# Order and queues of the opening loads, and a weight fold turned into 64-row passes, in a fused attention and feed-forward block

## The chip, the cores and the metric

The program runs on one core of one Trainium2 chip. The metric is the device time of one execution in microseconds (us). A profiled execution gives the trace; its span is the stretch that the trace covers. Engines are written PE (TensorE, matmul), PEld (TensorE weight load, which overlaps PE), ACT (ScalarE), DVE (VectorE), POOL (GpSimd) and SP (SyncE). Of these, SP and ACT issue DMAs here, each into a queue of its own; SPq and ACTq in the trace are those issues.

## The reference

x is 2048 tokens by 448. A layer norm of x feeds two branches, and the result is x plus both:

```
x = A_x;  xn = layernorm(x)
return x + A(xn, A_wqkv, A_w_phi, A_wo) + B(xn, B_w1, B_w2)

def A(x, wqkv, w_phi, wo):            # H = 16 heads of Dh = 28
    q, k, v = split(x @ wqkv)
    pq = einsum("bhsd,hdf->bhsf", q, w_phi);  pk = the same of k
    phi_q = concat(softmax(pq), softmax(-pq));  phi_k = the same of pk
    kv = einsum("bhsf,bhsd->bhfd", phi_k, v);  z = sum over s of phi_k
    num = einsum("bhqf,bhfd->bhqd", phi_q, kv);  den = einsum("bhqf,bhf->bhq", phi_q, z) + 1e-6
    return merge_heads(num / den) @ wo
def B(x, w1, w2): return silu(x @ w1) @ w2        # 448 -> 1792 -> 448
```

The head map w_phi (16 matrices of 28x28) acts on q and k only through the product wqkv times w_phi, so the kernel forms that product once, which is called the fold, and multiplies tokens by the folded weight.

## The kernel before, in words

Tokens are cut into 16 tiles of 128. The kernel does not run its loops on the engines directly: it records operations (`P.op`, `P.dma`), tracks what each reads and writes, and a list scheduler (L218) with a cost for every operation sets the order on each engine. That order is then emitted with semaphore waits. PE's order is fixed by hand: a head that is written out word by word in a `chain`, and after it the string `PLAN` (L334). In PLAN, `aF3@4` and `bF3` are the two halves of feed-forward block 3 into PSUM banks 4 and 5, `av2`, `ak2`, `aq2` the same for v, k and q of tiles 2 and 3, `f2@24` a part of the fold, `K0-2` the kv product, `M` its masking, `Y` and `F` with a small number the second feed-forward matmul of a tile, `U` the product of phi_q with kv, and `W`, `R`, `E` the output projection and store. Work of 64 rows is done as pairs, two matmuls in the two halves of the array into two banks.

**Opening loads (L505 to L555).** SP's queue issues x of tile 0, of tile 1, of tiles 2 and 3, then w1 columns 0 to 511 (two loads, called w1_0 and w1_0r here), the last rows of w1 columns 512 to 1023, x of tiles 4 to 7, the rest of w1, wv, x of tiles 8 to 11, and x of 12 to 15. ACT's queue issues the head map (Wp, 56 bytes a row) and then the main part of w1 columns 512 to 1023 (w1_512). The order on SP behind x of tiles 8 to 11 is written out in a chain (L931): three of the eight transposing loads of wqkv (wT_dma0 to 2, L580), x of 12 to 15, the transposes of normalised tiles 4 to 7 (xnT_dma5 and 7), the other five of wqkv, the transposes of tiles 8 to 15, w2 and wo.

**Head.** DVE normalises tiles 0 to 3 in the order of a chain (L893): statistics of tiles 0 and 1 come before the scale of tile 0. PE transposes them, ACT or DVE moves them back to SBUF, and PE starts feed-forward blocks 0, 1 and 2 tile by tile (L905 to L919). Tile 4 and later tiles are transposed by DMA. Blocks 5 and 6 of the next 512 tokens (F12, F13) are the first to read them.

**Fold (L568 to L597).** POOL spreads the head map into block-diagonal form, 112 rows by 4 times 112 (BDphi). For each of four row blocks of wqkv (kt), eight matmuls of 112 rows by 112 columns multiply transposed wqkv with it. `f2@24` does row blocks 2 and 3, `f0@24` row blocks 0 and 1, 16 matmuls each. For each kt, ACT copies the last column of each head (last27), and one DVE subtraction of 864 elements a partition writes Wqk without that column; the kernel uses that a softmax does not change under a common shift. The transposed wqkv lies in the space of Y_sb, which is written much later.

Of the kernel before, what the change touches and what calls it, by code (L numbers as in the profile page):

```python
# [140 lines left out]
class _Prog:  # L141
# [76 lines left out]
    def schedule(self):  # L218
# [55 lines left out]
        while done < n:  # L274
# [58 lines left out]
          ("pool", "pe"): 100.0}  # L333
PLAN = """aF3@4 bF3 aF6@0 aF4@2 bF4 bF6 av2@4 aF5@6 bv2 bF5 av0@2 aF12@0 aF13@4 bv0 bF12 bF13 aF11@6 bF11 f2@24 aF8@0 aF10@6 bF8  # L334
bF10 f0@24 aF9@0 aF7@6 bF9 bF7 ak2@4 bk2 av12@6 ak14@2 bv12 av10@0 bk14 bv10 ak4@4 av14@6 bk4 ak0@2 bv14 ak8@0 bk0 bk8
av6@6 Y2@5:1 Y2:9 Y2:4 ak6@2 av8@0 bv6 bv8 bk6 av4@6 ak10@4 bv4 bk10 ak12@2 aq4@0 bk12 K0-2 bq4 aq6@4 K2-4 bq6 aq8@2
K4-6 bq8 aq0@0 aF17@4 s4 K6-10 bq0 aF14@2 bF17 bF14 aF19@0 K10-12 bF19 aF16@4 K12-16 aF23@2 bF16 bF23 aF27@0 aF24@4 bF27
bF24 M aF20@2 aF25@0 bF20 aF15@4 bF25 aF26@2 aF22@6 bF26 aF18@0 s6 s8 bF22 bF15 bF18 aq2@6 aF21@2 aq10@4 bF21 bq2 aq12@0
bq10 bq12 F7@3:8 Y0@6:7 U9 Y1@5:6 F6@4:14 Y1:3 s0 F9@2:11 U6@1 Y1:5 U5 U7@0 Y0:7 F9:3 s2 Y3@1:10 Y3:4 W9 s10 s12 U10
U3@5 W6 F7:6 aq14@0 R9,6 bq14 U8 W7 F5@4:8 s14 F10@5:7 U0 F10:7 U11@6 U12@1 F5:6 U4@2 F4@0:10 W5 F8@7:12 W10 F4:4 F8:2  # L340
U2@1 W4 W0@6 W3@2 W8 R4,3 R8 R0,7,10,5 F13@1:14 F11@2:3 F12@6:4 F14@5:7 W2@3 U1@4 U13 F14:7 F11:2 F11:3 F12:1 F11:4 U14
F11:1 F11:1 W11 W1@4 F12:9 W12 U15 W13 W14 R14,12 R13,11 R1,2 F15@07:5 F15:5 F15:4 E15"""


def bass_parallel_sum__linear_kernel_hedgehog__dense_activation_silu__prompt_kernel(
# [12 lines left out]
    KP = 112  # L358
# [17 lines left out]
    with es:  # L376
        def sb(name, shape, dt):
            return es.enter_context(nc.sbuf_tensor(name, shape, dt))
# [12 lines left out]
        DQ = H * DF  # L391
        Wqk = sb("Wqk", [128, 2, 4, DQ], BF16)
        last27 = sb("last27", [128, 4, 2, H], F32)
        Wp = sb("Wp", [KP, G, DH], BF16)
        BDphi = sb("BDphi", [KP, G, KP], BF16)

# [23 lines left out]
        ones_bf = sb("ones_bf", [128, 128], BF16)  # L420
        ones4 = sb("ones4", [KP, 4], F32)
        mtmp = sb("mtmp", [KP, 4], F32)
        maskh = sb("maskh", [KP, 4], F32)
        mask2 = sb("mask2", [KP, 2], F32)
# [37 lines left out]
        def d_pool(n, per=1.0):  # L462
            return n * per + 120.0
# [35 lines left out]
        def load(dst, src, name, eng="sp", lat=1700.0):  # L499
            n = 2  # L500
            for _, cnt in list(dst.ap):
                n *= cnt
            P.dma(lambda e: e.dma_start(out=dst, in_=src), n / 280.0, writes=[dst], name=name, eng=eng, lat=lat)  # L503

        load(Wp[:], A_w_phi.rearrange("(g hl) d f -> (hl d) g f", g=G), "wphi", eng="act", lat=2500.0)  # L505
        memset(ones_bf[:], 1.0, 128, "ones")
# [5 lines left out]
        memset(ones4[:], 1.0, 4, "ones4")  # L512
        act(warm_act[:], ones_bf[:, 0:4], ACTF.Sqrt, 1750, "warm_act", table="sqrt")

        def block_mask(dst, w, n):
            tmp = mtmp[:, 0:n]
            P.op("pool", d_pool(4), lambda e: e.affine_select(tmp, ones4[:, 0:n], [[-w, n]], ALU.is_ge, 0.0,
                                                               base=0, channel_multiplier=1),
                 reads=[ones4[:]], writes=[tmp], name="mask1")
            P.op("pool", d_pool(4), lambda e: e.affine_select(dst, tmp, [[w, n]], ALU.is_ge, 0.0,  # L520
                                                               base=w - 1, channel_multiplier=-1),
                 reads=[tmp], writes=[dst], name="mask2")

        block_mask(maskh[:], DH, 4)

# [6 lines left out]

        def load_x(t0, t1):
            load(x_sb[:, t0:t1, :], xt[:, t0:t1, :], f"x{t0}", lat=1400.0)

# [4 lines left out]
        def load_w1(c0, c1, eng="sp"):  # L540
            load_rows4(w1_sb[:, :, c0:c1], B_w1, c0, c1, f"w1_{c0}", eng)

        load_x(0, 1)
        load_x(1, 2)
        load_x(2, 4)
        load(w1_sb[:, 0:2, 0:512], B_w1[0:256, 0:512].rearrange("(k p) f -> p k f", p=128), "w1_0")
        load(w1_sb[:, 2:4, 0:512], bass.AP(B_w1.tensor, B_w1.offset + 256 * FF, [[FF, 128], [64 * FF, 2], [1, 512]]), "w1_0r")
        load_w1(512, 1024, "act")
        load_x(4, 8)
        load_w1(1024, FF)  # L550
        load_rows4(wv_sb, A_wqkv, 2 * D, 3 * D, "wv")
        load_x(8, 12)
        load_x(12, 16)
        load(w2_sb[:], B_w2.rearrange("(f p) d -> p f d", p=128), "w2")
        for i in range(2):  # L555
# [9 lines left out]

        bd4 = BDphi[:].rearrange("p g (h f) -> p g h f", h=4)

        def fold():  # L568
            P.op("pool", d_pool(448, 2.0), lambda e: e.tensor_tensor(
                bd4, Wp[:, :, None, :].broadcast_to([KP, G, 4, DH]),  # L570
                maskh[:, None, :, None].broadcast_to([KP, G, 4, DH]), ALU.mult),
                reads=[Wp[:], maskh[:]], writes=[BDphi[:]], name="bdphi")

        def fold_loads():
            for a in range(8):
                dma_t(wT_sb[:, a, :], A_wqkv[:, a * KP:a * KP + 128], 600.0, f"wT_dma{a}", 1800.0 if a == 2 else 1310.0, sbuf=False)

        def fold_mms(k0, slots):
            mms = []
            for kt, fb in zip((k0, k0 + 1), slots):  # L580
                for qk in range(2):
                    wps = banks[fb + qk][:, 0:G * KP].rearrange("p (g c) -> p g c", g=G)
                    mms += [(wps[:, g, :], wT_sb[0:KP, qk * 4 + g, KS[kt]:KS[kt] + 128], BDphi[:, g, :], True, True) for g in range(G)]
            P.cur_slack = 400.0
            pe_mms(mms, "fold", dur=50.0 * len(mms))
            P.cur_slack = 0.0
            for kt, fb in zip((k0, k0 + 1), slots):
                src = psum[:, fb * 512:(fb + 2) * 512].rearrange("p (b c) -> p b c", b=2)[:, :, 0:D].rearrange("p b (h f) -> p b h f", f=DH)
                ref = last27[:, kt, :, :]
                act(ref, src[:, :, :, DF], ACTF.Identity, 32, "fold_ref")  # L590
                dst = Wqk[:, :, kt, :].rearrange("p b (h f) -> p b h f", f=DF)
                fold_sub(dst, src[:, :, :, 0:DF], ref)

        def fold_sub(dst, src, ref):
            P.op("dve", d_dve(2 * DQ), lambda e: e.tensor_tensor(dst, src, ref[:, :, :, None].broadcast_to([128, 2, H, DF]), ALU.subtract),
                 reads=[src, ref], writes=[dst], name="fold_sub")
# [119 lines left out]
        def proj_block(t, b0, is_k):  # L716
            fns = pair_block(b0, DQ, lambda i, kt, r: xnT[r, t + i, kt, :],
                             lambda i, kt, r: Wqk[r, int(is_k), kt, :], "k" if is_k else "q")

            def evac():  # L720
                E2 = ek(t, 2)[:, :, 0:2 * D] if is_k else eq(t, 2)
                src = psum[:, b0 * 512:(b0 + 2) * 512].rearrange("p (i c) -> p i c", i=2)[:, :, 0:DQ].rearrange("p i (h f) -> p i h f", f=DF)
                dst = E2.rearrange("p i (h s f) -> p i h s f", s=2, f=DH)
                for sg in range(2):
                    act(dst[:, :, :, sg, 0:DF], src, ACTF.Exp, 2 * DQ, "exp", scale=(1.0 if sg == 0 else -1.0), table="exp", okeys_w=["acttab"])
                E4 = E2.rearrange("p i (h f) -> p i h f", f=DH)
                R2 = Rec[:, int(is_k), t:t + 2, :]
                step = 2 if is_k else 1
                for i in range(0, 2, step):
                    sums(E4[:, i:i + step], R2[:, i:i + step, :], step)  # L730
                if is_k:
                    scale_rows(t, is_k)

            return *fns, evac
# [158 lines left out]
        chain("bnst0 bnag0 bnst1 bnag1 rstd0 xn0a xn0 rstd1 xn1 bnst2 bnag2 bnst3 bnag3 rstd2 xn2 rstd3 xn3 ev3".split())  # L893
        chain("wphi warm_act w1_512 ve0 ve1 ev0a ev0 ev1 ve2 ve3 ev2 silu_table".split())
        fold_loads()
# [24 lines left out]
        chain("ev3 bnst4".split())  # L920
        block_mask(mask2[:], 2 * DH, 2)
        memset(vaug[:, :, :, DH], 1.0, 2150, "vaug1")
# [6 lines left out]
        for t in range(8, NT):  # L929
            ln_tile(t)  # L930
        chain("x8 wT_dma0 wT_dma1 wT_dma2 x12 xnT_dma5 xnT_dma7 wT_dma3 wT_dma4 wT_dma5 wT_dma6 wT_dma7 xnT_dma9 xnT_dma11 xnT_dma13 xnT_dma15 w2 "  # L931
              "wo0 wor0 wo1 wor1".split())
# [18 lines left out]
        for word in PLAN.split():  # L951
# [10 lines left out]
            elif kind == "f":  # L962
                k0, slots = arg.split("@")
                fold_mms(int(k0), tuple(map(int, slots)))
            elif kind == "K":
# [141 lines left out]
```

The softmax here doesn't subtract the row's maximum and nothing guards it: scores larger than these inputs give would overflow.

## Time and profile before

| what | value |
|---|---|
| time before, median of 4 runs | 149.99 us |
| lowest and highest run | 149.33 and 151.0 us |
| the profiled execution's own time | 151.0 us |
| its span in the trace | 149.7 us |
| granted TensorE clock | 1.0 |
| HBM read, written | 6.56 MB, 1.84 MB |

The table's own-time row is one of the four runs, so 1.3 us of it lie outside the span and it is 1.0 us above the median. DVE is busy for 60% of the span, ACT for 47%, POOL for 48%. The busy time of POOL is concentrated in the middle, where it scales phi_k and phi_q. Lines of the page and the views give a start, a duration, the engine, the source line, the tiles written and read, and in brackets the idle time just before with what ended it. Times in the views count from the start of the span.

### The profile page before, as it was taken

How to read it: one execution, taken by the hardware profiler on the slowest of the kernel's cores; microseconds unless marked ns; L12 is line 12 of the kernel's file. 1: busy time of each engine (PE TensorE's matmuls, PEld its weight loads, DVE VectorE, ACT ScalarE, POOL GpSimd, SP SyncE). 2: the span in 40 equal slices, each digit the busy share in tenths (PEclk: the TensorE clock that was granted, in tenths of full speed). 3: DMA queues.
4: the chain of work that ended last, by engine and by line, in shares of the span. 5: the costliest groups of instructions: out<-in, count | busy, mean ns of one | idle time of the engine just before them, and what ended most of it. 6: DMA issues, size and time to landing. Idle time of an engine off the chain costs nothing.

```text
span 149.7 us, 3656 instructions
## 1 busy us (share of the span) xinstructions
PE 145.6 (97%) x1540; PEld 80.8 (54%) x1540; DVE 90.4 (60%) x189; ACT 70.8 (47%) x88; POOL 71.4 (48%) x82
## 2 busy tenths in 40 slices
PE   7899999999999999999999999999999999999994
PEld 7686444454554456566444444555545655455563
DVE  1839899344199949702997002999377902825284
ACT  3436775655999399969755769600003000000000
POOL 7105467701049999999699900599000800000000
PEclk9999999999999999999999999999999999999999
DMA  4999984899900000000078860038889348532325
GB/s 101 353 375 206 190 179 77 165 165 343 276 6 4 0 0 7 0 4 0 4 139 122 163 125 15 4 72 172 154 105 194 72 73 169 138 120 43 66 65 185
DMA packets 44352, 17.42 MB, mean 116 GB/s; under 512 B 36912, under 2 KB 43952, under 8 KB 44336
## 3 DMA queue, kind: packets, MB, share of 16 engines
q1 hardware_dynamic: 41168, 14.99, 48.4%
q10 hardware_dynamic: 3168, 2.20, 4.7%
q8 instruction: 12, 0.20, 0.6%
q14 instruction: 4, 0.03, 0.1%
HBM read 6.56 MB, written 1.84 MB: 56 GB/s over the span
## 4 chain that ended last, share of the span: by engine, by line
PE 92%; DMA 4%; SPq 1%; DVE 1%; issue 0%
PE psum L469 92%; DMA phT<-in_B_w_dram 4%; SPq L503 1%; DVE x_sb L855 1%; PE psum L484 0%
## 5 line engine op out<-in xcount | busy, mean ns | idle before, releaser
L469 PE MATMUL psum<-xnT,phT 64*128 64x512 bf16 (+1 forms) x428 | 46.9, 355 | 0.4
L469 PE MATMUL psum<-w_sb,hT 128*128 128x448 bf16 (+1 forms) x238 | 45.2, 342 | 0.0
L737 DVE TENSOR_REDUCE Rec<-Ek_sb 128x32 f32<-128x896 bf16 (+1 forms) x20 | 24.3, 1247 | 26.8 <-ACT Ek_sb L489 19.2
L773 POOL TENSOR_TENSOR RA<-Ek_sb,Rec 128x896 bf16<-128x896 bf16 x16 | 27.0, 1724 | 21.1 <-DVE Rec L738 19.7
L489 ACT ACTIVATE hT<-psum 128x1024 bf16<-128x1024 f32 x28 | 27.3, 1023 | 13.2 <-PE psum L469 13.2
L469 PEld LDWEIGHTS psum<-xnT,phT 64*128 64x128 bf16 (+1 forms) x428 | 21.8, 97 | 21.5 <-PE psum L469 1.7
L469 PEld LDWEIGHTS psum<-w_sb,hT 128*128 128x128 bf16 x238 | 22.3, 98 | 18.7 <-issue 1.5
L489 ACT ACTIVATE Ek_sb<-psum 128x864 bf16<-128x864 f32 x24 | 20.2, 932 | 17.4 <-DVE x_sb L855 16.1
L469 PE MATMUL psum<-Wqk,xnT 64*128 64x432 bf16 x224 | 23.7, 343 | 0.1
L747 POOL TENSOR_TENSOR Ek_sb<-Ek_sb,Rec 128x896 bf16<-128x896 bf16 x8 | 13.4, 1703 | 9.1 <-ACT phT L489 9.1
L469 PEld LDWEIGHTS psum<-Wqk,xnT 64*128 64x128 bf16 x224 | 10.4, 95 | 10.1 <-PE psum L469 0.8
L747 POOL TENSOR_TENSOR phT<-phT,Rec 128x896 bf16<-128x896 bf16 x8 | 13.4, 1706 | 0.0
L469 PE MATMUL psum<-wv,xnT 64*128 64x448 bf16 x112 | 12.7, 349 | 0.0
L602 DVE BATCH_NORM_STATS2 st<-x_sb 128x6 f32<-128x448 bf16 x16 | 9.7, 605 | 3.5 <-DMA x_sb<-in_A_x_dram 3.5
L469 PE MATMUL psum<-wo_sb,vaug 128*128 128x448 bf16 (+1 forms) x51 | 11.0, 341 | 0.0
L833 DVE TENSOR_SCALAR den<-psum 128x16 f32<-128x16 f32 x16 | 2.4, 157 | 13.4 <-PE psum L469 13.4
L840 DVE TENSOR_TENSOR vaug<-psum,rden 128x448 bf16<-128x448 f32 x16 | 9.8, 623 | 0.4
L489 ACT ACTIVATE vaug<-psum 128x896 bf16<-128x896 f32 x8 | 7.4, 934 | 5.1 <-PE psum L469 5.0
L617 DVE TENSOR_SCALAR RA<-x_sb,mv,rstd 128x384 bf16<-128x384 bf16 (+4 forms) x29 | 8.9, 344 | 1.4 <-POOL rstd L613 1.2
L855 DVE TENSOR_TENSOR x_sb<-psum,x_sb 128x448 bf16<-128x448 f32 (+1 forms) x13 | 7.1, 582 | 2.9 <-PE psum L469 2.9
L738 DVE RECIPROCAL Rec<-Rec 128x32 f32<-128x32 f32 (+1 forms) x24 | 8.6, 391 | 0.1
L469 PEld LDWEIGHTS psum<-wv,xnT 64*128 64x128 bf16 x112 | 5.5, 94 | 5.2
(51 smaller groups left out, 107.6 us busy)
## 6 DMA issues: line engine op xcount, KB each, us to landing
out_dram<-x_sb ACTq DMA_DIRECT2D x15, 112.0 KB, 1.8
w_sb<-in_B_w_dram SPq DMA_DIRECT2D x1, 1568.0 KB, 7.5
x_sb<-in_A_x_dram SPq DMA_DIRECT2D x3, 448.0 KB, 6.9
wo_sb<-in_A_wo_dram SPq DMA_DIRECT2D x2, 336.0 KB, 8.4
phT<-in_B_w_dram SPq DMA_DIRECT2D x1, 576.0 KB, 8.0
phT<-in_B_w_dram SPq DMA_DIRECT2D x2, 256.0 KB, 5.6
phT<-in_B_w_dram ACTq DMA_DIRECT2D x1, 384.0 KB, 4.6
wv<-in_A_wqkv_dram SPq DMA_DIRECT2D x1, 336.0 KB, 8.4
```

The lines of the kernel that those rows point to most:

```text
L469: r = e.matmul(dst, lhsT, rhs, start=st, stop=sp, skip_group_check=True)
L489: P.op("act", d_act(n), lambda e: e.activation(dst, src, func, scale=scale), reads=[src], writes=[dst], table=table, name=name, **keys)
L503: P.dma(lambda e: e.dma_start(out=dst, in_=src), n / 280.0, writes=[dst], name=name, eng=eng, lat=lat)
L602: P.op("dve", 590, lambda e: e.bn_stats(st6[:, t, :], xs), reads=[xs], writes=[st6[:, t, :]], name=f"bnst{t}", okeys_w=["ln"])
L617: P.op("dve", dur, lambda e: e.tensor_scalar(dst, x_sb[:, t, c0:c1], mv[:, t, 0:1], rstd[:, t:t + 1], ALU.subtract, ALU.mult), reads=[xs, ...
L737: P.op("dve", 50 + 967 * n, lambda e: e.tensor_reduce(R2, E4, AXL.X, ALU.add), reads=[E4], writes=[R2], name="Ssum")
L738: P.op("dve", 135 + 210 * n, lambda e: e.reciprocal(R2, R2), reads=[R2], writes=[R2], name="Rrec")
L747: P.op("pool", 1700, lambda e: e.tensor_tensor(E3, E3, Rk[:, :, None].broadcast_to([128, 32, DH]), ALU.mult), reads=[E3, Rk], writes=[E3], ...
L773: P.op("pool", 1700, lambda e: e.tensor_tensor(dst, Eq, Rq.rearrange("p (c j) -> p c j", c=CC)[:, :, :, None].broadcast_to([128, CC, 4, DH ...
L833: P.op("dve", 190, lambda e: e.tensor_scalar(den[:, uq, :], U3[:, :, DH], EPS_DEN, None, ALU.add), reads=[U3[:, :, DH]], writes=[den[:, uq ...
L840: P.op("dve", 620, lambda e: e.tensor_tensor(o3, U3[:, :, 0:DH], rden[:, uq, :, None].broadcast_to([128, H, DH]), ALU.mult), reads=[U3[:, ...
L855: P.op("dve", d_dve(cs.stop - cs.start), lambda e: e.tensor_tensor(res[:, cs], ob, addend[:, cs], ALU.add), reads=[ob, addend[:, cs]], wri ...
```

## The change

It does four things.

1. Tile 1 of x goes out on ACT's queue, as its first DMA; SP's queue starts with tile 0 and goes on to tiles 2 and 3. The main part of w1 columns 512 to 1023 moves from ACT's queue to SP's, behind w1_0 and w1_0r.
2. The head map is no longer loaded first on ACT's queue, but by four DMAs in SP's queue (one of 112 partitions with three pieces of 56 bytes each, three of 56 partitions with one piece), behind x of tiles 12 to 15 and ahead of xnT_dma5.
3. The fold is done in passes of 64 rows and 56 columns (two heads). wqkv is transposed by nine DMAs (NW = 9) whose columns overlap so that each half of a tile holds two whole heads. Each kt then takes nine matmuls in the low half of the array and seven in the high half, into two banks. Four words `f0`, `f3`, `f2`, `f1` of PLAN do one kt each. PW is 56. Every kt has two ACT copies and three DVE subtractions (54, 432 and 378 elements). POOL makes two smaller block-diagonal tiles and two more masks.
4. PLAN is new. The first fold word comes after six more pairs of feed-forward matmuls than before, and the order of Y, F, U, W and R words in the last third differs; the amount of that work does not.

```diff
-        load(Wp[:], A_w_phi.rearrange("(g hl) d f -> (hl d) g f", g=G), "wphi", eng="act", lat=2500.0)
...
         load_x(0, 1)
-        load_x(1, 2)
+        load_x(1, 2, "act")
         load_x(2, 4)
...
-        load_w1(512, 1024, "act")
+        load_w1(512, 1024)
...
         load_x(12, 16)
+        phi = A_w_phi.rearrange("h d f -> (h d) f")
+        P2 = 2 * DH
+        load(Wp[8:8 + KP, 0:3, :], phi[P2:P2 + 3 * KP, :].rearrange("(g p) f -> p g f", g=3), "wphi")
+        load(Wp[8:64, 3, :], phi[D - P2:D, :], "wphi1")
+        load(Wp[64:64 + P2, 3, :], phi[0:P2, :], "wphi2")
+        load(Wp0[0:P2, :], phi[0:P2, :], "wphi3")
...
         def fold_loads():
-            for a in range(8):
-                dma_t(wT_sb[:, a, :], A_wqkv[:, a * KP:a * KP + 128], 600.0, f"wT_dma{a}", 1800.0 if a == 2 else 1310.0, sbuf=False)
+            for i in range(NW):
+                c = max(0, KP * i - 64)
+                dma_t(wT(i), A_wqkv[:, c:c + 128], 600.0, f"wT_dma{i}", 1800.0 if i == 2 else 1310.0, sbuf=False)
...
-                    mms += [(wps[:, g, :], wT_sb[0:KP, qk * 4 + g, KS[kt]:KS[kt] + 128], BDphi[:, g, :], True, True) for g in range(G)]
+                mms.append((banks[b][:, PW * i:PW * i + PW], w[lo], BD[lo, (i - 1) % G, :] if i else BD0[:], i == 0, i == NW - 1))
+                if 0 < i < NW - 1:
+                    mms.append((banks[b + 1][:, PW * (i - 1):PW * i], w[hi], BD[hi, (i - 1) % G, :], i == 1, i == NW - 2))
...
-        chain("wphi warm_act w1_512 ve0 ve1 ev0a ev0 ev1 ve2 ve3 ev2 silu_table".split())
+        chain("x1 warm_act ve0 ve1 ev0a ev0 ev1 ve2 ve3 ev2 silu_table".split())
...
-        chain("x8 wT_dma0 wT_dma1 wT_dma2 x12 xnT_dma5 xnT_dma7 wT_dma3 wT_dma4 wT_dma5 wT_dma6 wT_dma7 xnT_dma9 xnT_dma11 xnT_dma13 xnT_dma15 w2 "
+        chain("x8 wT_dma0 wT_dma1 wT_dma2 x12 wphi wphi1 wphi2 wphi3 xnT_dma5 xnT_dma7 wT_dma3 wT_dma4 wT_dma5 wT_dma6 wT_dma7 wT_dma8 xnT_dma9 xnT_dma11 xnT_dma13 xnT_dma15 w2 "
```

The two PLAN strings up to the first k block, the old one first:

```
aF3@4 bF3 aF6@0 aF4@2 bF4 bF6 av2@4 aF5@6 bv2 bF5 av0@2 aF12@0 aF13@4 bv0 bF12 bF13 aF11@6 bF11 f2@24 aF8@0 aF10@6 bF8 bF10 f0@24 aF9@0 aF7@6 bF9 bF7 ak2@4
aF3@4 bF3 aF4@0 aF6@2 av2@6 bF4 bF6 aF5@4 av0@0 bv0 bF5 aF12@2 bv2 aF11@0 aF13@4 bF12 bF11 bF13 aF10@6 aF8@0 f0@2 f3@4 bF8 bF10 f2@2 aF9@0 f1@4 aF7@6 bF9 bF7 ak2@4
```

## The prediction

> **What bounds the kernel now.** I read the page's busy times and slices first, then the chain of work in order of time, then the timeline of the opening, and last the timelines of PE and of SP's queue where the change touches them.
>
> ```profile
> PE 145.6 (97%) x1540; PEld 80.8 (54%) x1540; DVE 90.4 (60%) x189; ACT 70.8 (47%) x88; POOL 71.4 (48%) x82
> ...
> PE   7899999999999999999999999999999999999994
> ```
>
> PE is busy in every slice but the first two and the last, so the only time to be won is PE work itself, the opening, and the end. The chain says where PE waited:
>
> ```profile
> 2.67 6.42 DMA phT<-in_B_w_dram
> 9.09 0.05 issue
> 9.14 0.98 PE psum L469 x8
> ...
> 26.91 9.64 PE psum L469 x102
> 36.55 0.04 issue
> 36.60 110.69 PE psum L469 x1184
> ```
>
> Columns are start, length and what. The last wait of PE on anything but itself ends at 9.14 us, with the load w1_0r (issued at 2.67). From there to 147.3 us PE has no gap worth a tenth: whatever a new order adds as a wait is paid in full, and whatever PE work goes is gained in full. The opening:
>
> ```profile
> 0.80 0.42 ACTq L503 DMA_DIRECT2D Wp<-in_A_w_phi_dram  x1
> ...
> 0.80 1.35 SPq L503 DMA_DIRECT2D x_sb<-in_A_x_dram  x3
> ...
> 1.31 0.45 ACTq L503 DMA_DIRECT2D phT<-in_B_w_dram  x1
> ...
> 4.36 0.63 DVE L602 BATCH_NORM_STATS2 st<-x_sb 128x6 f32<-128x448 bf16 x1 [0.32 <-DMA x_sb<-in_A_x_dram]
> ...
> 9.13 0.77 PEld L469 LDWEIGHTS psum<-xnT,phT 128*128 128x128 bf16 x8 [0.39 <-DMA phT<-in_B_w_dram]
> ```
>
> Two waits stand in the head: 0.32 us of DVE for tile 1 of x, ahead of the scale of tile 0, and 0.39 us of PE for w1_0r. The fold and the nearest thing to its new form, the 64-row kv product, on PE:
>
> ```profile
> 27.88 0.96 PE L469 MATMUL psum<-BDphi,Y_sb 112*128 112x112 bf16 x16
> 28.77 3.20 PE L469 MATMUL psum<-xnT,phT 64*128 64x512 bf16 x28
> ...
> 57.63 0.66 PE L469 MATMUL psum<-vaug,Ek_sb 64*128 64x58 bf16 x32
> 58.13 1.44 PE L469 MATMUL psum<-Wqk,xnT 64*128 64x432 bf16 x14
> ```
>
> The step from one start to the next is what PE pays: 0.89 us for 16 fold matmuls, 0.50 us for 32 kv matmuls. Last, SP's queue between the opening and the fold, with one issue from later on:
>
> ```profile
> 12.78 0.58 SPq L503 DMA_DIRECT2D x_sb<-in_A_x_dram  x1
> 15.33 3.54 SPq L560 DMA_TRANSPOSE xnT<-RA  x2
> 18.92 6.99 SPq L560 DMA_TRANSPOSE Y_sb<-in_A_wqkv_dram  x5
> ...
> 33.09 1.64 SPq L503 DMA_DIRECT2D wor_sb<-in_A_wo_dram  x1
> ```
>
> SP is idle from 13.36 to 15.33 (it waits for DVE's tile 5) and then issues without a break, 1.40 us a transposing load, until the last of the eight at 24.65.
>
> **The change part by part.**
>
> *Tile 1 on ACT's queue.* DVE's statistics of tile 1 can follow those of tile 0 at 4.04 instead of 4.36, as the chain has nothing else between. A DMA issued at 0.80 landed after 2.4 us (tile 0) or 2.5 us (the map, on this very queue); at 3.3 tile 1 is ahead of 4.04 by 0.7. So -0.32 us, which passes through scale, transposes and ACT's evacuation to the first real matmul (7.15, where PE waited 0.35 us for that evacuation). Its weights, w1_0, landed at 2.19 + 4.8 = 6.99 beside w1_512; with those 384 KB behind it, it is no limit at 6.8. The other end is 0: tile 0 shares the engines with 112 KB instead of 24.5 KB, and 88 KB more at the 319 GB/s and above that the trace shows from 3.6 us on is up to 0.28 us later. I take -0.30. The Trainium skill, "DMA: Bandwidth & Descriptors", section "Issuing engines are not separate DMA queues", speaks against this part: DMAs from SP and ACT run on the same engines and interleave, and two issuers save only issue time. By it tile 0 would pay for tile 1's bytes, the gain here would be about 0.05, and the whole sum 0.25 worse.
>
> *w1_512 behind w1_0r.* w1_0r landed at 9.09. With 384 KB fewer ahead of it, at the 362 GB/s of the window from 5 to 10 us, it comes 1.1 us sooner, at 8.0, and PE wants it at 9.13 - 0.39 - 0.30 = 8.44: the wait of 0.39 goes. Next late is w1_512 itself: PE gets there at about 9.4 (10.18 before, less 0.7), and the bytes up to its last part, which landed at 3.15 + 6.3 = 9.45, are the same as before. So -0.35, between -0.39 and 0 (if one late engine held w1_0r and holds its successor). Head together: -0.65.
>
> *The map loaded late, on SP.* Out of the opening it frees ACT's 0.42 us of issue, which hid nothing. In SP's queue four issues stand ahead of xnT_dma5. At the usual 0.42 to 0.58 us they take 2.0 us, 13.36 to 15.36, under the idle stretch that ended at 15.33; but DVE is now ready at 15.31 - 0.65, so the cover is used up to the last tenth. xnT_dma5 is issued at 15.36, xnT_dma7 at 16.8, and that one lands 4.0 us after issue (before: 17.13 + 4.0), so 20.8, plus the time of 504 small packets; 143 of them took 33% of the DMA engines for 0.3 us, so all take about 0.35 us: 21.2. F12, whose first weight load stood at 22.06, is now wanted at 21.4. Nothing is lost, with 0.2 to spare. The other end is that the issues cost 1.64 us each, as the one behind the big loads did; see the second rival. POOL waits for the map after the scale of tile 9 and then works about 0.7 us (0.93 for 448 elements before), so the scales of tiles 10 to 15 come some 1.5 us later; DVE was through with tiles 8 to 15 at 27.2, 2.0 us ahead of the first subtraction of the fold at 29.2, which covers it.
>
> *Nine transposing loads instead of eight.* xnT_dma7's issue ends at 18.5, five loads of 1.40 follow, and the ninth is issued at 25.5. The rows give 3.0 us (the last one) to 4.4 us (median) to landing: 28.5 to 29.9. PE reaches the first fold word at 27.88 - 0.65 + 12 matmuls at 0.112 (3.13 us for 28) = 28.6. So the wait is 0 to 1.3; near the lower row, because no bulk load is then in the queue: +0.45. The same 1.4 us pushes xnT_dma9 to 15, w2 and wo back; w2 landed at 39 and is first read at 47, and tile 15 at 33.5 for a use at 38, so this is hidden.
>
> *The fold on PE.* Before 2 x 0.89 = 1.78 us. After, per kt, nine pair passes (nine low, seven high beside them) at 0.50/16 = 31 ns: 0.28, four times 1.12. No change between full and half array is left around them; it is inside the 0.89. So -0.66, between -0.78 (64/32 x 0.50) and, if a pass of 56 columns cost what one of 112 does, 36 x 56 ns = 2.0, +0.2. The kv row has 58 columns and is the same form, so I stay with it. The skill's "TensorEngine Tiling (Array Packing)", "Instruction Overhead", gives a matmul about 60 cycles of overhead, the same latency for 1 column as for 60, and warns against shrinking a dimension that is already small. At its 60 cycles and 2.4 GHz a pass is 25 ns, the fold an estimated 0.90 us and the sum 0.2 better; the kv row shows 31 ns, and it decides.
>
> *Evacuation of the fold.* Eight ACT copies instead of four (0.14 us each in pairs) and DVE 3 x 4 subtractions: per kt the same 864 elements (2.02 us for two, so 1.01) and two more starts. DVE's sums took 1990 ns for 1792 elements and 1061 for 896, 1.04 ns an element; 864 of them are 0.90, so a start costs 0.11 and a kt 1.23. The last two words, f2 and f1, are copied by ACT only after the silu of F8 and F10. F8's second half ends 0.56 + 0.89 = 1.45 us after the first fold word, the two silu (0.97 each) at 3.5, the first copy at 3.65; with 2 x 1.23 DVE is done at 6.1 and, with 0.2 of signalling, k2 may go at 6.3. PE reaches k2, which reads Wqk and the bank of f1, after 1.12 + 44 x 0.112 = 6.05. Wait +0.25, between 0 and 0.6 (one silu more).
>
> *The rest of PLAN.* The same matmuls in another order, with the same two 64-row excursions in the last third. Before, none of its waits showed; I add 0.
>
> **Sum:** -0.65 - 0.66 + 0.45 + 0.25 = -0.61 us. The profiled execution's own 151.0 (span 149.7) becomes 150.4; it was 1.0 above the median of 149.99, from which the forecast is 149.4.
>
> **The rivals.**
>
> *All waits stay hidden.* The ninth load lands by 28.6 and Wqk is ready: -0.65 - 0.66 = -1.31, 148.7. For it: before, the eighth load landed at 27.65, 0.2 ahead of a fold at 27.88, and PE had no wait at all. Against it: the fold moved by 0.7 us and its last load by 0.85.
>
> *The transposes come late (slower).* If the four map issues cost more than 0.5 us each, xnT_dma5, xnT_dma7 and the six loads behind slide one for one. At 0.97 us (the issue at 32.08) xnT_dma7 lands at 22.7, F12 waits 1.3, the fold another 0.5: 150.7. At 1.64, xnT_dma7 lands at 25.4, waits of 4.0 and 0.5: 153.4. From a total wait of 1.3 us, some 0.85 us an issue, it is slower than before. I price it between them, at 152. For it: transposes are queued ahead, and issues at 8.67 took 2.33. Against: x of 12 to 15 was issued right behind three of them in 0.58.
>
> *The head does not move.* Tile 0 is slowed by its neighbour and the engine that held w1_0r holds w1_512 instead: head -0.05, rest as in the forecast: 150.0.
>
> **How the numbers follow.** The forecast 0.42, all hidden 0.25, late transposes 0.15, head unmoved 0.18. The forecast's own range is 148.8 to 149.9. To hold eight in ten it reaches from 148.5, which leaves out the better half of a quarter, to 151.0, which leaves out most of the late transposes. A measurement of this kernel tells about 1% from no change, 1.5 us. Faster than 148.5 takes under half of the all-hidden case and a tail of the forecast: 0.17. Slower than 151.5 takes most of the late transposes and a little from an unseen wait in the new PLAN: 0.14. Within 1%: 0.69.
>
> **What would show each step.** First real matmul at 6.8 instead of 7.15 and no wait for w1 at 8.4. Fold groups of 16 matmuls with 0.28 us from start to next start. The first fold word at about 29, with PE idle before it for a DMA; k2 at 35.1 instead of 35.8, with a short wait on DVE. Wrong would be PE idle before F12, a wait of more than 1.3 us ahead of the fold, or any gap of PE after 40 us; the last would mean that the new PLAN is what decides.

## The result, and the profile after

| | before | changed |
|---|---|---|
| median of the runs beside each other | 149.91 us (56 runs) | 151.11 us (34 runs) |
| lowest to highest | 149.23 to 151.86 | 149.90 to 152.27 |
| ratio, 95% interval | | 1.0064 [1.0044, 1.0083] |
| the profiled execution's own time, its span | 151.0, 149.7 | 149.72, 148.5 |

The changed kernel is 0.6% slower; the forecast was 0.4% faster. That is less than the 1% that the prediction called measurable, but the interval excludes no change. The two profiled executions say the opposite of the medians: that of before lay at the upper end of its runs, that of the changed kernel below every timed run. So a second profile of the changed kernel was taken (e4 below), and where the two differ both are given. The ratios leave out slow executions, those over some 1.5% above the fastest of their kernel, while the medians hold them: that matters for e12 below, with 5 of 12.

The page of the changed kernel, busy times and slices:

```profile
PE 143.5 (97%) x1572; PEld 79.4 (53%) x1572; DVE 91.5 (62%) x197; ACT 71.8 (48%) x92; POOL 71.5 (48%) x88
...
PE   7799999899999999999999999999999999999994
```

PE still fills the span, with 2 us less work, and still has little else than work to win. Its chain in order of time, from the fold on (start, length, what):

```profile
24.88 2.60 DMA wT<-in_A_wqkv_dram
27.48 0.14 issue
27.61 2.58 PE psum L476 x62
...
34.48 68.74 PE psum L476 x855
103.22 2.50 DMA vaug<-vaug
105.72 0.05 issue
105.76 35.04 PE psum L476 x255
...
142.46 2.96 DMA vaug<-vaug
145.42 0.05 issue
145.46 0.57 PE psum L476 x4
```

Before, this chain ran over PE alone from 9.14 us to the end. Now it leaves PE three times: for the ninth transposing load (wT) ahead of the fold, for a transposed attention output (vaug) at 105.7, and for another ahead of the last four matmuls. From 34.48, where the part behind the fold begins, to the last addition of DVE (146.06) it takes 111.58 us. The kernel before took 36.60 to 147.31 for the same part, 110.71. The SP queue ahead of the transposing loads:

```profile
11.80 0.58 SPq L510 DMA_DIRECT2D x_sb<-in_A_x_dram  x1
12.43 2.44 SPq L510 DMA_DIRECT2D Wp<-in_A_w_phi_dram  x4
14.92 2.65 SPq L577 DMA_TRANSPOSE xnT<-RA  x2
17.61 1.26 SPq L577 DMA_TRANSPOSE Y_sb<-in_A_wqkv_dram  x1
```

There is no idle time left in it: the four map issues take 2.44 us together here, 2.55 in the second profile and 3.17 in e1. The fold on PE, all four of its groups, and k2, the first matmul that reads its result:

```profile
27.61 0.39 PE L476 MATMUL psum<-BD,Y_sb 64*128 64x56 bf16 x16 [0.44 <-DMA wT<-in_A_wqkv_dram]
27.82 0.18 PE L476 MATMUL psum<-BD,wT 64*128 64x56 bf16 x1
27.84 0.34 PE L476 MATMUL psum<-BD,Y_sb 64*128 64x56 bf16 x13
...
28.08 1.89 PE L476 MATMUL psum<-xnT,phT 64*128 64x512 bf16 x15
29.75 0.42 PE L476 MATMUL psum<-BD,Y_sb 64*128 64x56 bf16 x15
30.01 0.18 PE L476 MATMUL psum<-BD,wT 64*128 64x56 bf16 x1
30.22 0.82 PE L476 MATMUL psum<-xnT,phT 64*128 64x512 bf16 x6
30.88 0.37 PE L476 MATMUL psum<-BD,Y_sb 64*128 64x56 bf16 x15
31.09 0.18 PE L476 MATMUL psum<-BD,wT 64*128 64x56 bf16 x1
31.14 2.55 PE L476 MATMUL psum<-xnT,phT 64*128 64x512 bf16 x22
33.69 1.69 PE L476 MATMUL psum<-Wqk,xnT 64*128 64x432 bf16 x14
```

From start to start the groups take 0.23, 0.24, 0.47 and 0.26 us, 1.2 in all, where the old fold took 1.78. The third is longer because the matmul behind it waits for ACT, whose silu ends at about 30.2. k2 too is late, by 0.17 us: matmul pairs start 0.22 apart, the last at 33.30, and k2 starts at 33.69, behind the end of DVE's last subtraction of the fold at 33.54. Neither shows as idle time of PE, since the ends of matmuls are modelled. From the first fold matmul to k2 it is 6.08 us, 44 matmuls of 0.108 between, so 1.33 for the fold with its waits; before it was 7.94 us with 56 between, so 1.90. That gain of 0.57 is real. Ahead of it stands the wait for wT: 0.44 us here, 1.0 in the second profile.

### The profile page after: what moved, and what is told of

Read it like the earlier page. It is cut to its first block, busy times and chain, and to the rows that moved or that the text cites. A ratio compares the mean times of both kernels' runs of the same rounds, so it can differ in the third digit from the quotient of the medians.

```text
span 148.5 us, 3741 instructions
## 1 busy us (share of the span) xinstructions
PE 143.5 (97%) x1572; PEld 79.4 (53%) x1572; DVE 91.5 (62%) x197; ACT 71.8 (48%) x92; POOL 71.5 (48%) x88
## 3 DMA queue, kind: packets, MB, share of 16 engines
q10 hardware_dynamic: 2448, 1.89, 4.2%
## 4 chain that ended last, share of the span: by engine, by line
PE 77%; DVE 8%; DMA 7%; SPq 5%; issue 1%; POOL 1%; ACT 0%
PE psum L476 76%; SPq L577 5%; DMA vaug<-vaug 4%; DVE st L637 3%; DVE RA L652 2%; DMA wT<-in_A_wqkv_dram 2%; DMA x_sb<-in_A_x_dram 2%; DVE mv L638 1%; PE psum L491 1%; DVE x_sb L890 1%; DVE vaug L875 0%; ACT xnT L496 0%; POOL rstd L648 0%; DVE xnT L500 0%; POOL ve L646 0%
## 5 line engine op out<-in xcount | busy, mean ns | idle before, releaser
L476 PE MATMUL psum<-xnT,phT 64*128 64x512 bf16 (+1 forms) x428 | 45.1, 350 | 0.3 <-ACT xnT L496 0.2
L496 ACT ACTIVATE hT<-psum 128x1024 bf16<-128x1024 f32 x28 | 27.3, 1023 | 10.9 <-PE psum L476 10.9
L476 PEld LDWEIGHTS psum<-xnT,phT 64*128 64x128 bf16 (+1 forms) x428 | 21.3, 95 | 20.0 <-PE psum L476 0.6
```

The costliest lines, as they stand in the source:

```text
L476: r = e.matmul(dst, lhsT, rhs, start=st, stop=sp, skip_group_check=True)
L496: P.op("act", d_act(n), lambda e: e.activation(dst, src, func, scale=scale), reads=[src], writes=[dst], table=table, name=name, **keys)
```

## The experiments

Two theories stood at first. **Queue:** SP's issues in the opening put the transposing loads late, and PE waits ahead of the fold. **PLAN:** the new order behind the fold costs time. Later came **clock** (the head's matmuls run at half speed in some executions) and **instruction loads** (described at e11). The last columns are from each profile: PE's wait for transposing loads up to the fold; the start of the part behind the fold; and from there to the last addition of DVE.

| run | median, runs | ratio, 95% interval | wait | start | rest |
|---|---|---|---|---|---|
| before | 149.91, 56 | | 0 | 36.60 | 110.71 |
| changed | 151.11, 34 | 1.0064 [1.0044, 1.0083] | 0.4 | 34.48 | 111.58 |
| e1 changed opening, old rest | 151.41, 6 | 1.0099 [1.0078, 1.0120] | 1.6 | 36.02 | 111.74 |
| e2 old opening, new rest | 150.29, 12 | 1.0024 [1.0007, 1.0041] | 0 | 35.15 | 110.72 |
| e3 old, queues of the change | 150.09, 12 | 1.0012 [0.9983, 1.0042] | 1.0 | 35.94 | 110.72 |
| e4 changed again | 150.88, 6 | 1.0065 [1.0049, 1.0081] | 1.0 | 35.32 | 111.53 |
| e5 changed, map on ACT | 149.78, 12 | 0.9983 [0.9945, 1.0022] | 0.5 | 34.81 | 111.32 |
| e6 e5, 44 warm-up | 149.64, 12 | 0.9983 [0.9944, 1.0022] | 1.2 | 35.36 | 111.58 |
| e7 before, 44 warm-up | 149.66, 12 | 0.9991 [0.9960, 1.0023] | 0 | 35.16 | 110.76 |
| e8 before, 20 warm-up | 151.07, 12 | 1.0077 [1.0037, 1.0117] | 0 | 36.39 | 110.71 |
| e9 e5, two wT earlier | 149.92, 12 | 1.0006 [0.9972, 1.0039] | 0 | 35.75 | 111.59 |
| e10 changed, four more loads | 151.84, 6 | 1.0137 [1.0076, 1.0199] | 2.0 | 36.36 | 111.54 |
| e11 e5, 76 short warm-up | 148.80, 12 | 0.9923 [0.9888, 0.9958] | 0 | 34.30 | 110.72 |
| e12 e9, 44 warm-up | 151.27, 12 | 1.0025 [0.9981, 1.0068] | 2.0 | 36.23 | 111.59 |
| e13 before, 76 short warm-up | 149.63, 12 | 1.0034 [0.9997, 1.0071] | 0 | 37.02 | 110.72 |
| e14 changed, 76 short warm-up | 150.29, 12 | 1.0038 [1.0004, 1.0072] | 0.7 | 35.33 | 110.96 |
| e15 e5, 19 long warm-up | 150.15, 12 | 1.0032 [1.0002, 1.0061] | 0.3 | 34.26 | 112.13 |

The kernel before measured 149.75 to 149.93 us beside them.

**e1 to e4: which half of the change.** e1 and e2 exchange PLAN behind the word `bk2`, the first k block:

```diff
# e1, in the changed kernel
-... ak2@4 bk2 av12@6 av10@0 ak14@2 bv12 bk14 bv10 ... F15@23:6 F15:8 E15
+... ak2@4 bk2 av12@6 ak14@2 bv12 av10@0 bk14 bv10 ... F15@07:5 F15:5 F15:4 E15
# e2, in the kernel before: the same exchange the other way
# e3, in the kernel before
-        load_x(1, 2)
+        load_x(1, 2, "act")
+        load(Wp[:], ..., "wphi", eng="act", lat=2500.0)    # was ahead of all others
-        load_w1(512, 1024, "act")
+        load_w1(512, 1024)
```

> The changed opening, queues and fold, with the old order of the PE plan from the word after the first k block on. Theory A, the new order in the last third waits for transposed attention outputs: those waits go and the gain of opening and fold stays, so about 1.0 us faster than before (ratio 0.993), and PE idles less than 0.3 us after 40 us. Theory B, the opening or the late transposes cost it in most runs: as slow as the changed kernel, ratio 1.006, with PE idle before the fold.

> The opening, queues and fold of before, with the new order of the PE plan from the word after the first k block on. Theory A: slower than before by the waits for the transposed outputs, 1.0 to 2.0 us (ratio 1.007 to 1.013). Theory B: as before, ratio 1.000 within 0.002.

> The kernel before with only tile 1 of x on ACT's queue, the map behind it there, and the main part of w1 columns 512 to 1023 in SP's queue. If the queues give what was forecast, 0.65 us faster (ratio 0.996). If the head is set by the clock of PE and not by the loads, the same as before on average, with the matmuls of the head at 107 ns in some runs and 56 ns in others.

> The changed kernel unchanged, for a second profile beside the others on one chip. The first profile took 149.7 us, below every timed run. Theory A: this profile shows the same waits for transposed outputs, of another length. Theory C, the runs differ by the clock of PE in the head alone: this profile has the head's 128-column matmuls at 107 ns where the first had 56, and the rest is the same to 0.2 us.

With the old rest the changed opening is no faster (e1, 151.41), and with the old opening the new rest costs 0.24% (e2). So the order alone is not what decides. e2's part behind the fold takes 110.72 us without a gap, as before; where its 0.24% comes from was not found. e1 brings a reading that the PLAN theory could not give: the old order too shows a vaug wait (0.8 us at 139.5) when the new opening stands ahead of it. So the opening does something to the far end of the kernel (e11 shows what; in e1 the load that PE waited for, 135.35 to 139.45, has an instruction load within it, 137.23 to 138.37). e3 wins nothing either: the head's queues alone were worth about zero, and PE waited 1.0 us at the fold. The profile names POOL's fill of the tile Ek_sb as the end of that wait, but the fold does not read Ek_sb. The last transposing load of wqkv landed at 27.10, and PE starts 0.13 us later, as it does behind wT in the changed kernel (27.48 to 27.61). So the wait was most likely for that load.

**e5: the map loads out of SP's queue.**

```diff
-        load(Wp[8:8 + KP, 0:3, :], phi[...]..., "wphi")
+        load(Wp[8:8 + KP, 0:3, :], phi[...]..., "wphi", "act")
...
-        chain("x1 warm_act ve0 ...
+        chain("x1 warm_act wphi wphi1 wphi2 wphi3 ve0 ...
-        chain("x8 wT_dma0 wT_dma1 wT_dma2 x12 wphi wphi1 wphi2 wphi3 xnT_dma5 ...
+        chain("x8 wT_dma0 wT_dma1 wT_dma2 x12 xnT_dma5 ...
```

> The changed kernel with one thing undone: the four map loads leave the SyncE queue and are issued on ScalarE, behind the load of tile 1 and the first table load, about 2.7 to 4.4 us, where ScalarE is idle until 4.3 us. The transposing loads then follow tiles 12 to 15 of x directly. Queue theory (the loss is SyncE's 2.4 to 3.2 us for issuing the four map loads, which puts the ninth transposing load late): xnT_dma5 is issued by about 12.5 to 13.5 us instead of 14.9 to 16.0, the wait of PE for wT (0.4 to 1.6 us ahead of the fold) is gone, the kernel is 0.4 to 1.6 us faster than the changed one, 149.6 to 150.3 us, no slower than before by more than 0.3%. Theory of the rest of the PLAN (the loss comes from PE's waits for transposed attention outputs behind 100 us): the wait ahead of the fold may go, but the kernel stays at 150.6 to 151.2 us. Theory of the clock (the loss is only that more executions have a slow head): the median stays at about 150.9 us too, with the two groups of times as far apart as they were.

149.78 us, 1.1 to 1.3 below the changed kernel's two medians, as the queue theory had it. SP's queue:

```profile
11.97 0.58 SPq L510 DMA_DIRECT2D x_sb<-in_A_x_dram  x1
13.82 3.77 SPq L577 DMA_TRANSPOSE xnT<-RA  x2
17.64 7.13 SPq L577 DMA_TRANSPOSE Y_sb<-in_A_wqkv_dram  x5
24.81 1.26 SPq L577 DMA_TRANSPOSE wT<-in_A_wqkv_dram  x1
```

SP is idle again from 12.55 to 13.82; it now waits for DVE. The two pair loads go out from 13.82 instead of 14.92 (changed), 15.49 (e4) and 16.04 (e1), but in e5 their two issues take 3.77 us instead of 2.65. The other five transposing loads start at 17.64, and at 17.25 and 17.22 in e11 and e15, which have the same queues. With the map in SP's queue they start at 17.61, 18.18 (e4) and 18.73 (e1). So the map's issues cost this row nothing in the best execution and up to 1.1 us in others. A wait of 0.5 us ahead of the fold is left in e5's profile, which the expectation had ruled out. Not all of e5's gain need be the queue's: between the profiles of e4 and e5, 0.5 us of it lies ahead of the part behind the fold and 0.2 in that part, where e5 has no vaug wait ahead of the last four matmuls.

**e10: the same cost doubled.**

```diff
+        for i in range(4):
+            load(Wp_x[64 * (i % 2):64 * (i % 2) + 56, i // 2, :], phi[0:56, :], f"more{i}")
```

> The changed kernel with the suspected cost doubled: four more small loads of the map (into a tile that only a late memset touches) in SyncE's queue behind its four, computation as before. Queue theory (0.6 to 0.8 us for each such issue, and nothing idle in the queue behind it): the ninth weight load is issued and lands 2.4 to 3.2 us later than in the changed kernel, PE waits 2.8 to 4.8 us ahead of the fold, and the kernel is 2.4 to 3.2 us slower than the changed one: about 153.3 to 154.1 us. The forecast's own price (0.5 us each, partly hidden): 151.5 to 152.5 us. If the queue does not bind: 150.9 to 151.1 us.

```profile
12.46 2.95 SPq L511 DMA_DIRECT2D Wp<-in_A_w_phi_dram  x4
15.46 1.68 SPq L511 DMA_DIRECT2D Wp_x<-in_A_w_phi_dram  x4
17.18 2.65 SPq L580 DMA_TRANSPOSE xnT<-RA  x2
19.87 6.66 SPq L580 DMA_TRANSPOSE Y_sb<-in_A_wqkv_dram  x5
```

It moved the time in the right direction and by a third of the amount: 151.84 us, 0.7 to 1.0 above the changed kernel instead of 2.4 to 3.2. The extra four took 0.42 us each where the four ahead of them took 0.74. But that excess is no price of each issue: the first two of the map's four issues hold it (1.08 and 0.51 us in the changed kernel, 1.29 and 0.81 in e10), and the third and fourth take 0.33 and 0.39 in each of the five profiles with the map in this queue. It is paid once, so four more issues did not double it. PE waits 1.0 us for xnT at block F12 and 1.0 us for wT, which is the second rival's mechanism.

**e9 and e12: two wT loads in SP's idle time.** Both have the map on ACT, and e12 has 44 warm-up matmuls as well.

```diff
-        chain("... x12 xnT_dma5 xnT_dma7 wT_dma3 wT_dma4 wT_dma5 ...
+        chain("... x12 wT_dma3 xnT_dma5 wT_dma4 xnT_dma7 wT_dma5 ...
```

> The kernel with the map loads on ScalarE, and two of the transposing weight loads (wT 3 and 4) issued in the two stretches where SyncE there waits for VectorE (12.6 to 13.8 us ahead of the pair load of tiles 4 and 5, and ahead of that of tiles 6 and 7). Queue theory (the fold's start is set by the end of SyncE's row of issues, whatever fills it): the ninth weight load is issued about 2 us earlier, about 22.5 us instead of 24.8 to 25.6, PE does not wait for wT, and the kernel is 0.3 to 1.2 us faster than with the map loads on ScalarE alone (149.78 us): 148.6 to 149.5 us. If the landing is bound by the DMA engines and not by the issues: wT 8 lands at 27 us or later again, 149.6 to 149.9 us. Price of the move: the pair loads may land later, and then PE waits behind 20 us for xnT.

> As the kernel with two transposing loads issued earlier, and 44 warm-up matmuls in place of 38. Best version by the theories of queue and clock: 148.6 to 149.3 us, below both kernels. If the gain of either is spent on another wait, 149.5 us or more.

Both missed: 149.92 and 151.27 us, with ratios that tell neither from the kernel before. e12's chain shows why:

```profile
17.52 5.20 DMA xnT<-RA
22.73 0.05 issue
22.77 9.18 PE psum L476 x124
```

PE now waits 2.0 us for the pair load of tiles 6 and 7, which needs 5.20 us from its issue where the trace of before shows 4.0. The wait ahead of the fold is gone, and a longer one stands ahead of F12. The expectation had named this price of the new order, but the order alone does not make it: with the same order the pair load took 3.58 us in e9, and in e12 a load of instructions (20.16 to 21.89, see e11) lies within its flight. e9's profile has no such wait, but its head ran at the slow clock, so that PE came 1.6 us later (block F3 at 14.77 instead of 13.16 in e11). What the order costs without that load was not tried.

**e6, e7, e8: the clock of the head.** The edit is the number of warm-up matmuls on PE, `range(38)`.

> As the kernel with the map loads on ScalarE, and 44 warm-up matmuls on PE in place of 38, so that the warm-up ends at about 5.8 us at 107 ns each, where the first transposes were ready at 5.5 to 5.8 us. Clock theory (some executions run the head's 128-column matmuls at 107 ns until about 9.9 us, because no window of the clock was filled; that costs them up to 1.6 us): fewer executions of the slow group, the median 0.2 to 0.6 us below that of the kernel with 38, the highest time under 151.0 us. If the clock plays no part: within 0.15 us of the kernel with 38, with the same spread.

> The kernel before with 44 warm-up matmuls in place of 38, nothing else. Clock theory: about a third of its executions were in a slow group (150.6 to 151.9 us); with 44 that group shrinks, and the median falls by 0.1 to 0.4 us to about 149.6 us. If the clock plays no part: 149.9 us, ratio 1.000 within 0.1%, with the two groups as they were.

> The kernel before with 20 warm-up matmuls in place of 38. The warm-up then ends at about 3.2 us, and PE is idle for 2.5 us before the first transposes. Clock theory: the head's matmuls run at 107 ns in every execution until some window is filled, about 9 to 10 us, and the median goes to the slow group's 150.6 to 151.4 us (ratio 1.005 to 1.010), with one group of times in place of two. If the clock of the head plays no part: 149.9 us, ratio 1.000.

PE's timeline of e8, the first real matmuls, and after that of e7:

```profile
5.61 1.26 PE L484 MATMUL psum<-ident,RA 128*128 128x128 bf16 x8 [2.23 <-DVE RA L617]
6.68 2.77 PE L469 MATMUL psum<-xnT,phT 128*128 128x128 bf16 x24
```

```profile
5.75 0.44 PE L484 MATMUL psum<-ident,RA 128*128 128x128 bf16 x4 [0.76 <-DVE RA L617]
...
7.17 1.51 PE L469 MATMUL psum<-xnT,phT 128*128 128x128 bf16 x24 [0.36 <-DMA phT<-in_B_w_dram]
```

The same 24 matmuls take 2.77 us in one and 1.51 in the other, though the page of e8 grants nine tenths of the clock or more in every slice. With 20 warm-up matmuls every run is long (150.41 to 152.19); with 38, 7 of the 35 runs beside them are over 151 us; with 44 none of 12 is (up to 150.53 in e7, 150.59 in e6). The kernel before with 76 short ones (e13) has 4 of 12 over 151. The median gain of 44 is small: 0.9991 [0.9960, 1.0023] for before, and 0.14 us between e6 and e5. The Trainium skill, "TensorE: Matmul & The Clock Gate", section "What's actually happening", says that the array runs at half clock until a free-running window of some 3.4 us has been busy, so that the point of change depends on where the first matmul falls. e8 and the slow head of before agree with it.

**e11, e13, e14, e15: where PE's instructions are loaded.** The trace has DMA packets of kind "instruction": loads of 16 KB on queue q8, twelve in the changed kernel's span, each on one DMA engine for 0.9 to 1.4 us (up to 1.7 in other runs). That is one for each 262 of the 3144 records of PE and PEld. By the skill's "Trainium Architecture — The Big Picture", "The software stack", an instruction has 64 bytes, and a load would hold an estimated 256. In the changed kernels one falls at 100.7 (changed), 104.0 (e4) or 101.0 us (e5), among the four transposes of attention outputs; with the old opening the nearest ones are at 90.1 and 108.4 (e2). To shift the loads without touching the work, the warm-up was cut into more or fewer pieces:

```diff
-        for i in range(38): ... e.matmul(banks[3][:, 0:128], ones_bf[:], ones_bf[:], ...)
+        for i in range(76): ... e.matmul(banks[3][:, 0:64], ones_bf[:], ones_bf[:, 0:64], ...)   # e11, e13, e14
+        for i in range(19): ... e.matmul(banks[3][:, 0:256], ones_bf[:], ones2[:], ...)          # e15
```

> The kernel with the map loads on ScalarE, and the warm-up as 76 matmuls of 64 columns in place of 38 of 128, which is 76 more instructions for PE (a matmul and a weight load each) in about the same time. It tests what makes PE wait for a transposed attention output near 104 to 107 us in the changed kernel and in its variants, and not in the old opening with the same order. Theory of the instruction loads (a 16 KB load of PE's instructions takes one DMA engine for 0.9 to 1.7 us, near 101 to 104 us in the changed kernels, near 108 us in the other, and holds up the piece of the transposing load that is due on that engine): the load near 101 us moves to about 96 us, the wait of PE for vaug near 106 us (0.2 to 0.7 us) is gone, and the time falls by 0.2 to 0.5 us from 149.78. Rival (the wait comes from the order of PE's work or from the number of loads in flight): the wait stays, 149.8 us. A warm-up that fills the clock's window worse would show as a slow head and cost up to 1.2 us.

> The kernel before with the warm-up as 76 matmuls of 64 columns in place of 38 of 128, nothing else. Theory of the instruction loads: the kernel before shows no wait of PE behind 40 us that a moved load could take away, so that nothing is gained there: 149.7 to 150.2 us, ratio 0.998 to 1.002. Theory of the clock (the form of the warm-up itself gave the 1.0 us of the run with 76 short ones): the kernel before gains as well, about 149.0 to 149.3 us.

> The changed kernel, its map loads in SyncE's queue as they are, with the warm-up as 76 matmuls of 64 columns. Two causes of about 1 us each, the queue and the instruction loads, that add up: 149.8 to 150.2 us, the wait for vaug near 106 us gone, the wait for wT ahead of the fold still there (0.4 to 1.6 us). If the two are one cause (with the instruction loads moved, the queue of SyncE has room enough): 148.8 to 149.2 us. If moving them only helps with the map loads on ScalarE: 150.8 to 151.1 us.

> The kernel with the map loads on ScalarE (149.78 us with 38 warm-up matmuls of 128 columns, 148.80 with 76 of 64), now with 19 of 256 columns: the same busy time of the warm-up, and 38 instructions fewer for PE, so that each load of its instructions comes 38 instructions later. Theory of the instruction loads: the load near 101 us moves to about 103 us, still among the four transposing loads of 99 to 105 us, the wait for vaug near 106 us stays or grows (0.2 to 1 us), and the time is 149.6 to 150.3 us. Theory of the warm-up's form (any other form than 128 columns helps, or the order of instructions plays no part): 148.8 to 149.2 us.

DMA activity of the changed kernel from 98 to 106 us, in 40 slices of 0.2 us:

```profile
DMA  9999999979950408999300001099930049960009
GB/s 215 225 212 212 223 216 183 208 140 210 214 118 3 82 17 178 200 188 30 0 5 9 9 9 12 12 179 198 211 56 0 0 86 220 212 133 4 0 13 186
...
q8 instruction: 1, 0.02, 1.1%
...
vaug<-vaug SPq DMA_TRANSPOSE x4, 2.9
```

and of e11 from 98 to 104.5 us:

```profile
DMA  9999999999999200069992000599930005999300
GB/s 255 238 216 216 216 219 205 187 215 199 219 214 195 40 0 0 0 117 219 214 208 49 0 0 0 107 211 214 219 56 0 0 0 101 216 213 217 61 0 0
...
vaug<-vaug SPq DMA_TRANSPOSE x4, 2.5
```

In e11 the four transposes go through as four blocks at some 215 GB/s, 2.5 us from issue to landing. In the changed kernel there are 1.2 us (slices 21 to 26) at 5 to 12 GB/s, a sixteenth or less of 215. That fits one engine still at the piece that was held up by the load, which lasted from 100.7 to 102.1, while the transposes behind it stand; the view does not name the engine. The two transposes in flight during the load took 4.03 and 3.39 us to landing. The four issues take 6.02 us instead of 5.13. In e11 the load fell at 95.9 us, as expected, and the chain is PE's alone again:

```profile
27.45 2.58 PE psum L476 x62
...
34.30 110.69 PE psum L476 x1184
145.00 0.02 issue
145.02 0.77 DVE x_sb L890 x2
```

e15 shifts the load the other way, to 103.3 us, and the wait grows:

```profile
106.34 1.31 PE L477 MATMUL psum<-wo_sb,vaug 128*128 128x448 bf16 x6 [1.24 <-DMA vaug<-vaug]
```

Its rest takes 112.13 us, the longest of all, and 1.4 longer than in e11, which starts it at the same time (34.26 and 34.30) with the same work in the same order. e13 shows that the short warm-up gives the kernel before nothing, 1.0034 [0.9997, 1.0071]. e14 keeps the map in SP's queue: the wait near 106 is gone and 0.7 us of wait is left in the opening, now ahead of F12. Its 150.29 is 0.1 above the range for two costs that add: from the changed kernel's 150.88 to 151.11 it gains 0.6 to 0.8, from e14 to e11 another 1.5. The vaug wait ahead of the last four matmuls (0.3 us) is in the profiles of changed, e4 and e14, in which a load of 8 KB on q14 falls at 143.1 to 143.8 us; in e5 and e11 that load comes at 148.5 and 147.4, and there is no wait. That it is the cause was not tried.

The opening is not free of these loads either. In every one of the 17 profiles an issue in the row of transposing loads (15 to 26 us) that overlaps a 16 KB load takes 1.5 to 2.8 us, where most take 1.3: in the changed kernel 2.03 us at 21.51 (load from 21.18 to 22.47), in e14 2.09 for the second pair load (load from 17.45 to 18.59), so that its other five start at 19.18. e6 has the queues of e5 and starts these five at the same time (17.63), yet with an issue of 2.78 us among them its ninth goes out at 25.64 instead of 24.81, and PE waits 1.2 us instead of 0.5. So the wait ahead of the fold is made of the map's issues and of an instruction load; no run took the second out of this row.

e11 is the version that beats both kernels: 0.9923 [0.9888, 0.9958].

## Why the prediction was wrong, point by point

- **The base.** "The profiled execution's own 151.0 ... becomes 150.4; it was 1.0 above the median, from which the forecast is 149.4." The profiled execution was 1.0 above because its head ran at 107 ns a matmul: e7, the same kernel with a fast head, starts the part behind the fold at 35.16 instead of 36.60 and takes the same 110.7 for it. With the clock up, PE reaches the fold 1.4 us earlier (e2's fold at 26.44 with the old opening, 27.88 in the profile). In the kernel before the transposing loads come earlier with it, because SP waits for DVE ahead of them (the last is issued at 23.23 in e2, 24.65 in the profile). In the changed kernel the map's issues fill that stretch of SP, so a faster head does not bring the loads forward. A wait that a slow head hides is open in a fast one, so subtracting 1.0 from the sum was not allowed.
- **The head, -0.65: a term that was mis-sized.** Tile 1 landed in time for its statistics to follow tile 0's at once (4.09), and the wait for w1 went, as forecast. But tile 0 took a median of 2.6 us to land in the twelve profiles with tile 1 on ACT's queue and 2.3 in the five without: the 0.28 that the forecast had as its other end was paid. Among heads at the fast clock the first real matmul moved from 6.99 (e2) to 6.37 us, but PE's transposes for tile 2 only from 8.33 (e2) and 8.52 (e7) to between 8.06 and 8.29 (nine profiles), as DVE's scale of tile 2 hardly moved (7.79 in e2, 7.64 here). So some 0.2 us was won. e3, with just these queues, is 1.0012 [0.9983, 1.0042].
- **The map on SP's queue: the step that failed.** The forecast had four issues of 0.42 to 0.58 us, 2.0 together, hidden in an idle stretch of 2.0 us: "Nothing is lost, with 0.2 to spare." They took 2.00 (e14), 2.44 (changed), 2.55 (e4), 2.95 (e10) and 3.17 us (e1), and the stretch to hide them in is at most 1.3 us with the new opening (e3, e5, e6; less in e11 and e15) where the old one has 1.8 to 2.0 (before, e2, e7). So the transposing loads went back, by up to 1.1 us. e5, which takes just these four away, is 1.1 to 1.3 us faster. The second rival had the mechanism, with its break-even at 0.85 us an issue; the kernel was slower below that.
- **The wait ahead of the fold, +0.45.** 0.44, 1.0 and 1.6 us in the three profiles with this opening and these loads: the range of 0 to 1.3 was nearly right, the middle not. An instruction load in the row has a part in it (e6), which the forecast did not reckon with.
- **The fold on PE, -0.66, and evacuation, +0.25.** Together -0.41 was forecast and -0.57 measured (1.33 for 1.90). A group takes 0.23 to 0.26 us where nothing holds it up, 26 ns a pass; the row of 58 columns (31 ns) was too dear a model. The skill's "TensorEngine Tiling (Array Packing)", "Instruction Overhead", from which the prediction estimated 0.90 for the four, came nearer. The short wait of k2 for DVE was there as forecast, 0.17 us instead of 0.25; the 0.24 us behind the third group, for ACT, was not in the sum.
- **"Before, none of its waits showed; I add 0": the second failed step.** The rest is 0.8 to 0.9 us longer in the changed kernel. It is not the new order (e2 has 110.72) but the number of PE instructions ahead of it, which moves the instruction loads among the transposes of attention outputs (e11, e15).

With neither wait, e11 comes to 148.80, near the 148.7 of the rival "all waits stay hidden". That is partly luck: between the profiles of e7 and e11 some 0.3 us were won ahead of the fold and 0.57 at it, where the rival had 0.65 and 0.66. Of the changed kernel's +1.2 us over before, the runs price the map in SP's queue at 1.2 (e5) and the shift of the instruction loads at 1.0 (e5 to e11), against a gain of 1.1 (e11 to before). The part of e11's gain that lies ahead of the fold (0.5 of 1.1 us between the profiles of e5 and e11) was not separated into clock, queue and instruction loads.

## What to carry to other kernels

Before costing an edit from one profile, look at where that execution stands among the runs and why: if its head ran slow, waits are hidden in it that the others have. An issue in a queue that feeds a row of transposing loads is to be priced by rows at the same place in the queue, and "hidden in idle time" holds only while the price stays under that time in every execution, the ones with the shortest idle time too. A change of the instruction count moves instruction loads everywhere behind it; when a DMA wait appears or grows, near or far, compare the places of those loads before blaming the order of the work.

## What the runs showed of the hardware that was not expected

- A 16 KB load of instructions keeps one DMA engine for 0.9 to 1.7 us, and transposing loads in flight meanwhile land later: 4.03 and 3.39 us in the changed kernel instead of 2.5. In all 17 profiles an issue of SP's row of transposing loads that overlaps such a load takes 1.5 to 2.8 us, where most take 1.3 (some pair loads take up to 2.1 without one).
- Four small DMA issues on SP took 2.0 to 3.2 us (e14, e1). The excess lay in the first two (1.09 and 1.24 us in e1); the third and fourth took 0.33 and 0.39 in all five profiles, and four more behind them 0.42 each (e10).
- The head's matmuls can run at half rate while the clock row grants nine tenths or more (before, e8); the times of the matmuls tell (24 in 2.77 or 1.51 us). In e13 the row did show it (0.65 from 7 to 10 us): there 8 matmuls took 0.61 us, and the 16 after them 1.89, so the clock also fell back after it had been up.
